# Reordered SwiGLU forward pass, other DMA queues and moved PSUM copies in a fused recurrent-attention and SwiGLU training step

## The chip, the core and the metric

The kernel runs on one core of a Trainium2 chip. The metric is the device time of one execution in microseconds (us): 5259.43 us, the median of three runs of the kernel before (5244.72 to 5269.86). The profiled execution has a span of 5258.0 us; all windows below are counted from its start.

Names: PE is TensorE, DVE is VectorE, ACT is ScalarE, POOL is GpSimd, SP is SyncE. SP, ACT and POOL start the DMA transfers; "the sync queue" is that of SP, "the scalar queue" that of ACT, "the GpSimd queue" that of POOL.

## What is computed

A training step: the output of one layer and the gradients of all its inputs. Cut to what matters:

```python
def f(x, mem0, Wq, Wk, Wv, Wo, w1, w3, w2):
    xn = layernorm(x)                       # 2048 x 640
    s = A(xn, mem0, Wq, Wk, Wv, Wo)         # recurrent attention
    g = silu(B(xn, w1, w3, w2))             # SwiGLU, hidden width 1728
    return x + s * g

def A(x, mem, ...):                         # 64 segments of 32 tokens, 32 heads of 128
    for seg in x:
        h = concat(mem, seg)                # 8 + 32 rows
        o = Wo(softmax(mask(q(h) @ k(h).T)) @ v(h))
        mem, out = o[:8], o[8:]             # the memory goes on to the next segment

def B(x, w1, w3, w2):
    return (silu(x @ w1) * (x @ w3)) @ w2

out, vjp = jax.vjp(f, ...)                  # returned: out and vjp(grad_out), nine gradients
```

All arrays are bfloat16. The 64 segments are a chain in both directions: each step of the forward and of the backward loop needs the 8 memory rows of the step before it.

## The kernel before

[...] The stages, in time: layer norm and SwiGLU forward (with the first V rows at its end), the first K and Q rows, the forward loop, a projection stage, the lead-in of the backward loop, the backward loop, and the weight gradients.

SwiGLU forward: four blocks of 512 tokens. `hidden` makes one 128-row chunk of the hidden layer (14 to a block), `up` the output rows of the block before.

```python
def fetch(blk):                     # 512 normalised rows, turned by DMA on the sync queue
    xnT = io.tile([P, DC, BLK], BF16, name="xnT_b", tag="xnT_b")
    for i in range(2):
        turned_load(k, xnT[...], k.XN[...])
    xnTs.append(xnT)

def hidden(blk, fc):
    pg = ps.tile([P, BLK], F32, name="pg", tag="pg")     # 2 PSUM buffers each
    pu = ps.tile([P, BLK], F32, name="pu", tag="pu")
    ...                                                   # 5 + 5 matmuls of 128x512
    sig = wk.tile(...)                                    # pool wk: bufs=2
    nc.scalar.activation(sig[:fsz], pg[:fsz], ACT.Sigmoid)
    nsig = wk.tile([P, BLK], BF16, name="nsig", tag="nsig", bufs=1)
    nc.scalar.activation(nsig[:fsz], pg[:fsz], ACT.Sigmoid, scale=-1.0)
    ut = wk.tile(..., bufs=3)
    nc.scalar.copy(ut[:fsz], pu[:fsz])
    sl = wk.tile(..., bufs=3)
    nc.vector.tensor_tensor(sl[:fsz], pg[:fsz], sig[:fsz], ALU.mult)
    nc.vector.tensor_tensor(hBT[:fsz, fc, :], sl[:fsz], ut[:fsz], ALU.mult)
    ds = wk.tile(..., bufs=3)
    nc.vector.tensor_tensor(ds[:fsz], nsig[:fsz], sl[:fsz], ALU.mult)
    nc.vector.tensor_tensor(ds[:fsz], sig[:fsz], ds[:fsz], ALU.add)
    nc.gpsimd.dma_start(k.SLT[...], sl[:fsz])
    nc.gpsimd.tensor_tensor(ds[:fsz], ds[:fsz], ut[:fsz], ALU.mult)
    nc.gpsimd.dma_start(k.DUT[...], ds[:fsz])

def hidden_out(blk):                # the whole hidden block, 1.7 MB
    nc.gpsimd.dma_start(k.HB[...], hBT[:, 0:FC - 1, :]) ...
```

The layer norm of the last three quarters of the rows (`ln_stats`, `ln_rstd`, `ln_rows`) is done between the chunks of block 0.

The first K and Q rows: 48 groups of two 112x512 tiles, with a copy by DVE and one by ACT into one staging tile of 224 KB, and a store of it. The weights Wq and Wo are loaded meanwhile on the scalar queue.

```python
# pool b0s: bufs=2
def first_rows(k, ps, stage, xs, off, W, dst, x0, cg, ...):
    for b in range(2):
        ...                                              # 5 matmuls of 112x512
        k.copy(st[:, s0:s0 + 512], pb[:], eng='vs'[b])   # 'v' is DVE, 's' is ACT
        if w == 512 or b == 1:
            nc.sync.dma_start(dst[...], st[:])
```

The fold that ends each step of both loops (the projection's partial sums lie in two halves of one PSUM bank), and what stands around it in the backward loop:

```python
def fold_add(k, pm, pool, lo="flo"):
    up = pool.tile([64, 160], F32, name="fup", tag="fup")
    nc.scalar.copy(up[:], pm[64:128, 0:160])
    lw = pool.tile([64, 160], F32, name="flo", tag=lo)
    nc.vector.tensor_copy(lw[:], pm[0:64, 160:320])
    nc.vector.tensor_tensor(fs[:, 0:160], pm[0:64, 0:160], up[:], ALU.add)
    nc.vector.tensor_tensor(fs[:, 160:320], pm[64:128, 160:320], lw[:], ALU.add)

WARM = dict(G4=1, G5=1)             # matmuls without use, to keep PE from pausing

def chain(t, gap):                  # one backward step; gap(...) puts other work in
    packed_half(k, bA, gox, WoT, 0)                      # 20 matmuls
    k.copy(sg[:, 0:512], bA[:], eng='s')
    packed_half(k, bB, gox, WoT, 1)
    k.copy(sg[:, 512:1024], bB[:], eng='v')
    packed_sel(k, pg, sg, 0)
    gap("W0")                                            # turn(t, 0): 8 transposes, 3 ACT copies
    packed_sel(k, pg, sg, 1)
    ...                                                  # gmT <- pg, two DVE copies
    gap("W1")                                            # turn(t, 1)
    for a in range(2):
        nc.tensor.transpose(pgo[:, a, :], gmT..., k.ident[:])
    nc.scalar.copy(gOst[:], pgo[:])
    dprob_m(0)                                           # 16 small matmuls
    gvT = gkv(1, gOst, bdP)                              # 2 matmuls with gOst, DVE
    ...
    fs = fold_add(k, pm, ch, "gstg")
    gap("G4")
    pt = fold_turn(k, bC, fs)                            # 6 small matmuls
    gap("G5")
    nc.vector.tensor_copy(goxs[(t - 1) % 2][:, :, 0:8], pt[:])   # what the next step starts from
```

The lead-in of the backward loop goes through 19 units of the same side work before the loop starts; in it the sync queue also turns Wq (5.2 MB, four DMA transposes) and two tiles of GS.

Of the kernel before, what the change touches and what calls it, by code (L numbers as in the profile page):

```python
# [16 lines left out]
P = 128  # L17
# [312 lines left out]
def fold_add(k, pm, pool, lo="flo"):  # L330

    nc = k.nc
    fs = pool.tile([64, 320], BF16, name="fsum", tag="fsum")
    up = pool.tile([64, 160], F32, name="fup", tag="fup")
    nc.scalar.copy(up[:], pm[64:128, 0:160])
    lw = pool.tile([64, 160], F32, name="flo", tag=lo)
    nc.vector.tensor_copy(lw[:], pm[0:64, 160:320])
    nc.vector.tensor_tensor(fs[:, 0:160], pm[0:64, 0:160], up[:], ALU.add)
    nc.vector.tensor_tensor(fs[:, 160:320], pm[64:128, 160:320], lw[:], ALU.add)
    return fs  # L340
# [19 lines left out]
def first_rows(k, ps, stage, xs, off, W, dst, x0, cg, nb=112, tag="b0pb", w=1024):  # L360

    nc = k.nc
    for b in range(2):
        c0 = cg * 1024 + b * 512
        if w == 512 or b == 0:
            st = stage()
        pb = ps.tile([nb, 512], F32, name="b0pb", tag=tag)
        for dc in range(k.DC):
            nc.tensor.matmul(pb[:], xs[:, dc, x0 - off:x0 - off + nb], W[:, dc, c0:c0 + 512],
                             start=(dc == 0), stop=(dc == k.DC - 1))  # L370
        s0 = b * 512 if w == 1024 else 0
        k.copy(st[:, s0:s0 + 512], pb[:], eng='vs'[b])
        if w == 512 or b == 1:
            nc.sync.dma_start(dst[x0:x0 + nb, cg * 1024 + (b * 512 if w == 512 else 0):cg * 1024 + b * 512 + 512], st[:])
# [21 lines left out]
def first_part(k, Wv, Wk_, Wq, Wo, kTs, vt, hxs, rest):  # L396
    nc, tc = k.nc, k.tc
    DC, H, HD = k.DC, k.H, k.HD
    with tc.tile_pool(name="b0", bufs=1) as io, tc.tile_pool(name="b0s", bufs=2) as stp, \
# [9 lines left out]
        for i, tt in enumerate(kTs + hxs + rest + [vt]):  # L409
            nc.gpsimd.memset(tt[:], 0.0)  # L410
        nc.gpsimd.dma_start(k.m_rows(k.HRO, 0), k.mem0)
# [21 lines left out]
        for W, dst in ((Wk_, k.KX[:, :]), (Wq, k.QVX[:, 0])):  # L433
            for x0 in range(0, k.NB0, 112):
                for cg in range(4):
                    if n % 2 == 0 and fetch:
                        nc.scalar.dma_start(*fetch.pop(0))
                    first_rows(k, ps, lambda: stp.tile([112, 1024], BF16, name="b0st", tag="b0st"), xs, 0, W, dst, x0, cg)
                    if n >= 26 and n % 2 == 0 and (n - 26) // 2 < 9:
                        i = (n - 26) // 2  # L440
                        if i > 0:
                            kturn(i - 1)
                        if i < 8:
                            kload(i)
                    if n == 44:
                        for i in range(2):
                            nc.sync.dma_start(vt[64 * i + 8:64 * i + 40, :], k.QVX[0:32, 1, 2048 * i:2048 * i + 2048])
                    n += 1
# [511 lines left out]
def phase4_Abwd(k, out2, WoT, WvT, WkT, WqT, later):  # L960
# [3 lines left out]
    with tc.tile_pool(name="gst", bufs=1) as st, tc.tile_pool(name="gchain", bufs=1) as ch, \  # L964
# [25 lines left out]
        WARM = dict(G4=1, G5=1)  # L990
# [53 lines left out]
        def chain(t, gap):  # L1044
# [20 lines left out]
            k.copy(sg[:, 0:512], bA[:], eng='s')  # L1065
            packed_half(k, bB, gox, WoT, 1)
            k.copy(sg[:, 512:1024], bB[:], eng='v')
# [13 lines left out]
            nc.scalar.copy(gOst[:], pgo[:])  # L1081
# [68 lines left out]
        def ld(tl, qd, eng=None):  # L1150
# [17 lines left out]
            (nc.gpsimd if early else nc.sync).dma_start(  # L1168
                qv[nx:n], k.QVM[t0:t0 + ns, :, qd // 2, :, 512 * (qd % 2):512 * (qd % 2) + 512].rearrange("t r i c -> (t r) i c"))
            k.load_x(qv, 0, k.x_src(tl, "qv", c0, c0 + 512), nc.sync)  # L1170
            k.load_x(gor, 0, k.g_src(tl, c0, c0 + 512), nc.scalar if early and i > 3 else nc.sync)
            nc.sync.dma_start(Pr[0:n], k.PR[tl][:, h0:h0 + 4, :])
# [46 lines left out]
        def gmem(tl, qd):  # L1219
# [12 lines left out]
            nc.gpsimd.dma_start(k.GXP[tl, :, qd, 0:ns], ks[:].rearrange("p s i h m -> p s i (h m)"))  # L1232
# [393 lines left out]
def phase12_ln_Bfwd(k: K, Wv, Wk_):  # L1626
# [6 lines left out]
    with tc.tile_pool(name="bw", bufs=1) as wp, tc.tile_pool(name="bio", bufs=2) as io, \  # L1633
# [29 lines left out]
        def ln_rows(tt):  # L1663
            xt = xts.pop(tt)
            nc.vector.tensor_scalar(xt[:], xt[:], mv[:, tt, 0:1], k.rstd_all[:, tt:tt + 1], op0=ALU.subtract, op1=ALU.mult)
            nc.gpsimd.dma_start(k.XN[tt * P:(tt + 1) * P, :], xt[:])
# [3 lines left out]
        def fetch(blk):  # L1670
            xnT = io.tile([P, DC, BLK], BF16, name="xnT_b", tag="xnT_b")
            for i in range(2):
                turned_load(k, xnT[:, :, i * BLK // 2:(i + 1) * BLK // 2], k.XN[blk * BLK + i * BLK // 2:blk * BLK + (i + 1) * BLK // 2, :])
            xnTs.append(xnT)

        def hidden(blk, fc):
# [11 lines left out]
            nsig = wk.tile([P, BLK], BF16, name="nsig", tag="nsig", bufs=1)  # L1688
# [3 lines left out]
            sl = wk.tile([P, BLK], BF16, name="sl", tag="sl", bufs=3)  # L1692
            nc.vector.tensor_tensor(sl[:fsz], pg[:fsz], sig[:fsz], ALU.mult)
            nc.vector.tensor_tensor(hBT[:fsz, fc, :], sl[:fsz], ut[:fsz], ALU.mult)
            ds = wk.tile([P, BLK], BF16, name="ds", tag="ds", bufs=3)
            nc.vector.tensor_tensor(ds[:fsz], nsig[:fsz], sl[:fsz], ALU.mult)
            nc.vector.tensor_tensor(ds[:fsz], sig[:fsz], ds[:fsz], ALU.add)
            nc.gpsimd.dma_start(k.SLT[fc * P:fc * P + fsz, cols], sl[:fsz])
# [3 lines left out]
        def up_ld(blk, ti):  # L1702
            tt = TB * blk + ti
            Gt = wk.tile([P, D], BF16, name="Gt", tag="Gt")
            nc.scalar.dma_start(Gt[:], k.G[tt * P:(tt + 1) * P, :])
# [35 lines left out]
        for w, src in ((w1s, k.w1), (w3s, k.w3)):  # L1741
            nc.scalar.dma_start(w[:, :, 0:512], src.rearrange("(dc p) f -> p dc f", p=P)[:, :, 0:512])
        for tt in range(TB):
# [4 lines left out]
        fetch(0)  # L1748
        for w, src in ((w1s, k.w1), (w3s, k.w3)):
            nc.sync.dma_start(w[:, :, 512:F], src.rearrange("(dc p) f -> p dc f", p=P)[:, :, 512:F])  # L1750
        for tt in range(TB, 3 * TB):
            ln_ld(tt)
        nc.scalar.dma_start(w2s[:, 0:FC - 1, :], k.w2[0:(FC - 1) * P, :].rearrange("(c p) d -> p c d", p=P))
        nc.scalar.dma_start(w2s[0:fszs[-1], FC - 1, :], k.w2[(FC - 1) * P:F, :])
        for blk in range(NBLK):
            for fc in range(FC):
                hidden(blk, fc)
                if blk in (1, 2) and fc % 3 == 1:
                    W, src = ((Wv, k.A_Wv), (Wk_, k.A_Wk))[blk - 1]
                    nc.scalar.dma_start(W[:, fc // 3, :], src.rearrange("(dc p) h e -> p dc (h e)", p=P)[:, fc // 3, :])  # L1760
                if blk == 0:
                    g, m = fc // 4 + 1, fc % 4
                    if g < 4:
                        if m < 2:
                            ln_stats(TB * g + 2 * m)
                            ln_stats(TB * g + 2 * m + 1)
                        else:
                            if m == 2:
                                ln_rstd(TB * g, TB * g + TB)
                            ln_rows(TB * g + 2 * m - 4)  # L1770
                            ln_rows(TB * g + 2 * m - 3)
                        if fc == 3:
                            for tt in range(3 * TB, NT):
                                ln_ld(tt)
                    if fc == 9:
                        fetch(1)
                    if fc == 13:
                        k.x_rows(k.HRO, k.XN, nc.sync)
                elif fc == 0:
                    hidden_out(blk - 1)  # L1780
                    for ti in range(2):
                        up_ld(blk - 1, ti)
                elif fc < 9 and fc % 2 == 0:
                    up(blk - 1, fc // 2 - 1)
                    if fc < 6:
                        up_ld(blk - 1, fc // 2 + 1)
                elif fc == 9:
                    fetch((blk + 1) % NBLK)
        hidden_out(NBLK - 1)
# [292 lines left out]
```

## Time and profile before

| stage | window, us | length, us | PE busy, us | DMA share |
|---|---|---|---|---|
| layer norm, SwiGLU forward until its first matmul | 0 to 24 | 24 | 0.30 | 0.78 |
| SwiGLU forward, four blocks | 24 to 264 | 240 | 184.07 | 0.73 |
| last `up` rows and first V rows, wait for the next stage | 264 to 350 | 86 | 68.47 | 0.46 |
| first K and Q rows | 350 to 484 | 134 | 116.09 | 0.55 |
| forward loop and its tail | 484 to 1878 | 1394 | 1215.11 | 0.52 |
| projection stage | 1878 to 1994 | 116 | 107.50 | 1.00 |
| lead-in of the backward loop | 1994 to 2136 | 142 | 53.23 | 0.80 |
| backward loop | 2136 to 3340 | 1204 | 1081.87 | 0.65 |
| weight gradients and the rest | 3340 to 5258 | 1918 | 1793.13 | 0.58 |

The table is from the view of busy time by window. PE busy is the sum of the matmul records in the window, which overlap one another a little; DMA share is the mean busy share of the core's 16 DMA engines. A row is read by the distance between its length and PE's busy time: where they lie close, PE sets the pace of the stage; where they lie apart, something else makes PE wait, and the view of waits for that window says what.

### The profile page before, as it was taken

How to read it: one execution, taken by the hardware profiler on the slowest of the kernel's cores; microseconds unless marked ns; L12 is line 12 of the kernel's file. 1: busy time of each engine (PE TensorE's matmuls, PEld its weight loads, DVE VectorE, ACT ScalarE, POOL GpSimd, SP SyncE). 2: the span in 40 equal slices, each digit the busy share in tenths (PEclk: the TensorE clock that was granted, in tenths of full speed). 3: DMA queues.
4: the chain of work that ended last, by engine and by line, in shares of the span. 5: the costliest groups of instructions: out<-in, count | busy, mean ns of one | idle time of the engine just before them, and what ended most of it. 6: DMA issues, size and time to landing. Idle time of an engine off the chain costs nothing. (4 is left out here: it accounts for less than half of the span.)

```text
span 5258.0 us, 160316 instructions
## 1 busy us (share of the span) xinstructions
PE 4619.8 (88%) x64317; PEld 2931.1 (56%) x64587; DVE 2241.9 (43%) x7236; ACT 1691.0 (32%) x4828; POOL 1960.6 (37%) x3309
## 2 busy tenths in 40 slices
PE   5778888888889874789999999789999999999999
PEld 2445555555555452455555555556665566657675
DVE  6623555555565522444444454323332233311361
ACT  3422455555555431223333333212322223200000
POOL 5620344444444402344444444423442334401340
PEclk9899999999999886899999999899999999999999
DMA  7754555555555488566776666645654355549783
GB/s 220 198 161 128 146 158 162 164 162 158 160 156 159 134 177 166 164 192 191 197 200 186 189 191 170 142 100 127 144 123 101 100 131 141 131 138 239 169 197 94
DMA packets 1042847, 836.70 MB, mean 159 GB/s; under 512 B 596361, under 2 KB 925005, under 8 KB 1040099
## 3 DMA queue, kind: packets, MB, share of 16 engines
q1 hardware_dynamic: 813748, 538.36, 39.3%
q0 software_dynamic: 125488, 222.36, 15.2%
q10 hardware_dynamic: 102867, 65.71, 4.9%
q8 instruction: 510, 8.36, 0.7%
q14 instruction: 234, 1.92, 0.1%
HBM read 463.32 MB, written 306.24 MB: 146 GB/s over the span
## 5 line engine op out<-in xcount | busy, mean ns | idle before, releaser
L1474 PE MATMUL wg<-gr,hr 128*128 128x512 bf16 x2352 | 525.3, 382 | 20.8 <-DVE dST L1398 14.5
L1453 PE MATMUL g<-w,ghacc 128*128 128x320 bf16 x3072 | 450.5, 305 | 0.0
L1474 PEld LDWEIGHTS <-hr 128*128 128x128 bf16 x2400 | 235.6, 98 | 302.7 <-issue 29.1
L1453 PEld LDWEIGHTS <-ghacc 128*128 128x128 bf16 x3072 | 299.4, 100 | 116.0
L306 PEld LDWEIGHTS <-hx 128*32 128x32 bf16 x7680 | 182.8, 98 | 175.2 <-issue 23.1
L713 POOL DMA_DIRECT2D OR<-xv x163 | 92.7, 569 | 483.7 <-ACT xv L712 378.9
L90 DVE CAST wgo<-wg 128x512 bf16<-128x512 f32 x72 | 47.5, 688 | 525.2 <-issue 249.8
L90 DVE CAST stg<-bank 128x512 bf16<-128x512 f32 x256 | 177.1, 692 | 199.4 <-PE bank L306 194.1
L325 PEld LDWEIGHTS <-gkv 128*8 128x8 bf16 x8192 | 188.2, 92 | 103.9 <-issue 3.0
L664 ACT ACTIVATE xP<-xsp,xnm 120x120 bf16<-120x120 f32 (+1 forms) x704 | 240.6, 376 | 8.4 <-DVE xnm L660 5.1
L1185 POOL DMA_DIRECT2D VTD<-gvT x176 | 129.6, 743 | 297.2 <-ACT gvT L1184 262.1
L1422 POOL DMA_DIRECT2D GSP<-grs x48 | 25.6, 538 | 523.0 <-ACT grs L1414 507.8
L92 ACT CAST wgo<-wg 128x512 bf16<-128x512 f32 x48 | 25.8, 589 | 573.3 <-PE wg L1474 573.3
L325 PE MATMUL gbank<-WvT,gkv 128*8 128x320 bf16 x4096 | 208.0, 358 | 0.2
L675 POOL TENSOR_TENSOR xP<-xP,xrz 120x480 bf16<-120x480 bf16 x163 | 161.8, 993 | 117.8 <-ACT xP L664 79.2
L1462 DVE TENSOR_TENSOR ghacc<-ghacc,g 128x320 f32<-128x320 f32 x192 | 93.7, 488 | 238.3 <-PE g L1453 238.3
L1414 ACT CAST gr<-r6p 120x512 bf16<-120x512 f32 x160 | 94.0, 587 | 302.0 <-PE r6p L1407 300.8
L1214 DVE SCALAR_TENSOR_TENSOR gdS<-gdp,Dx,gPr 120x120 bf16<-120x120 f32 (+1 forms) x680 | 183.0, 332 | 0.0
L325 PE MATMUL bank<-Wo,oTm 128*32 128x320 bf16 x4032 | 182.0, 336 | 0.3 <-DVE oTm L582 0.2
L1232 POOL DMA_DIRECT2D GXP<-gks x176 | 102.5, 582 | 208.8 <-ACT gks L1230 200.9
L243 POOL DMA_DIRECT2D r<-GOS x256 | 144.5, 568 | 71.8 <-PE r6p L1407 21.9
L539 DVE COPY vt<-stg 8x512 bf16<-8x512 bf16 x512 | 161.9, 316 | 20.9 <-ACT stg L92 13.2
(339 smaller groups left out, 10968.1 us busy)
## 6 DMA issues: line engine op xcount, KB each, us to landing
QVS<-stg SPq DMA_DIRECT2D x128, 256.0 KB
gqv<-QVS SPq DMA_DIRECT2D x108, 192.0 KB
vTt<-VTD SPq DMA_DIRECT2D x64, 320.0 KB
VTD<-gvT POOLq DMA_DIRECT2D x168, 120.0 KB, 4.0
DSR<-gdS POOLq DMA_DIRECT2D x168, 120.0 KB, 3.4
dS<-DSR SPq DMA_DIRECT2D x168, 120.0 KB
P<-PR SPq DMA_DIRECT2D x168, 120.0 KB
gPr<-PR SPq DMA_DIRECT2D x164, 120.0 KB
```

The lines of the kernel that those rows point to most:

```text
L90: return nc.vector.tensor_copy(out, in_)
L243: eng.dma_start(d, src if src.shape[0] > 1 else src[0])
L306: k.nc.tensor.matmul(bank[32 * g:32 * g + 32, :], x[:, dc, :], W[:, dc, c0:c0 + 512], start=(dc == 0), stop=(dc == k.DC - 1), tile_positio ...
L325: k.nc.tensor.matmul(pm[p0:p0 + nq, 0:320], x[:, h, :], W[:, h, 320 * b:320 * b + 320], start=(first and i == 0), stop=(last and i == 15), ...
L539: nc.vector.tensor_copy(vt[p0:p0 + 8, c0:c0 + 512], sv[32 * g:32 * g + 8, b * 512:(b + 1) * 512])
L664: nc.scalar.activation(Pb[0:n, j, 0:n], sp[0:n, j, :], ACT.Exp, bias=nmx[0:n, j:j + 1], scale=k.scale, accum_out=Z[0:n, j:j + 1])
L675: eng.tensor_tensor(Pb[0:n, :, 0:n], Pb[0:n, :, 0:n], bc_last(rz[0:n], n), ALU.mult)
L1185: nc.gpsimd.dma_start(k.VTD[tl][:, :, h0:h0 + 4, :], vTq[:])
L1214: nc.vector.scalar_tensor_tensor(dS[0:n, j, 0:n], dp[0:n, j, :], Dx[0:n, j:j + 1], Pr[0:n, j, 0:n], op0=ALU.subtract, op1=ALU.mult)
L1232: nc.gpsimd.dma_start(k.GXP[tl, :, qd, 0:ns], ks[:].rearrange("p s i h m -> p s i (h m)"))
L1453: nc.tensor.matmul(pg[:], ring[:, i, j, r0:r0 + P], Ws[qd][i][:, j, 320 * h:320 * h + 320], start=(i == 0 and j == 0), stop=(i == 2 and j ...
L1474: nc.tensor.matmul(accs[dc][:], hr[:, tl, dc * P:(dc + 1) * P], grs[i][:, tl, :], start=(tl == 0), stop=(tl == NF - 1))
```

## The change

The change has five parts.

1. **SwiGLU forward.** The first block's rows are turned by PE (`turn_first`) and copied by ACT instead of being stored and turned by DMA. The layer norm of a block is done in the block ahead of it, for all blocks, instead of all in block 0. `nsig` gets two buffers, `sl` and `ds` four. The stores of `sl`, and the loads of w2, Wv, Wk and G, go to the sync queue; the stores of `ds` and of the hidden block stay on the GpSimd queue.
2. **First K and Q rows.** Three staging tiles instead of two, the stores on the GpSimd queue, and most of the clearing of tiles by POOL moved from ahead of the stage to between its stores.
3. **fold_add.** One ACT copy of 320 columns replaces an ACT copy and a DVE copy of 160 each.
4. **Backward loop.** The two copies of `sg` change engines, `gOst` is copied by DVE, and the unused matmul at G5 is gone.
5. **Lead-in.** Its loads of Q, V and P rows go to the GpSimd queue, its loads of `gor` all to the sync queue, its stores of GXP to the sync queue.

The aim is to take waits of PE away at the start of the kernel and in the chains of both loops.

```diff
-def fold_add(k, pm, pool, lo="flo"):
+def fold_add(k, pm, pool, tag="fup"):
-    up = pool.tile([64, 160], F32, name="fup", tag="fup")
-    nc.scalar.copy(up[:], pm[64:128, 0:160])
-    lw = pool.tile([64, 160], F32, name="flo", tag=lo)
-    nc.vector.tensor_copy(lw[:], pm[0:64, 160:320])
-    nc.vector.tensor_tensor(fs[:, 0:160], pm[0:64, 0:160], up[:], ALU.add)
-    nc.vector.tensor_tensor(fs[:, 160:320], pm[64:128, 160:320], lw[:], ALU.add)
+    up = pool.tile([64, 320], F32, name="fup", tag=tag)
+    k.nc.scalar.copy(up[:], pm[64:128, 0:320])
+    for c in (0, 160):
+        k.nc.vector.tensor_tensor(fs[:, c:c + 160], pm[0:64, c:c + 160], up[:, c:c + 160], ALU.add)
 ... first_part
-    tc.tile_pool(name="b0s", bufs=2) as stp
+    tc.tile_pool(name="b0s", bufs=3) as stp
-        for i, tt in enumerate(kTs + hxs + rest + [vt]):
+        for tt in hxs:
             nc.gpsimd.memset(tt[:], 0.0)
+        zero = [kTs[0]] + [vt, kTs[1]] + rest
-                    first_rows(k, ps, ..., xs, 0, W, dst, x0, cg)
+                    first_rows(k, ps, ..., xs, 0, W, dst, x0, cg, q=nc.gpsimd)
+                    if zero:
+                        nc.gpsimd.memset(zero.pop(0)[:], 0.0)
 ... backward loop
-        WARM = dict(G4=1, G5=1)
+        WARM = dict(G4=1)
-            k.copy(sg[:, 0:512], bA[:], eng='s')
+            k.copy(sg[:, 0:512], bA[:], eng='v')
-            k.copy(sg[:, 512:1024], bB[:], eng='v')
+            k.copy(sg[:, 512:1024], bB[:], eng='s')
-            nc.scalar.copy(gOst[:], pgo[:])
+            nc.vector.tensor_copy(gOst[:], pgo[:])
 ... its lead-in
-            (nc.gpsimd if early else nc.sync).dma_start(
+            q = nc.gpsimd if early else nc.sync
+            q.dma_start(
                 qv[nx:n], k.QVM[...])
-            k.load_x(qv, 0, k.x_src(tl, "qv", c0, c0 + 512), nc.sync)
-            k.load_x(gor, 0, k.g_src(tl, c0, c0 + 512), nc.scalar if early and i > 3 else nc.sync)
-            nc.sync.dma_start(Pr[0:n], k.PR[tl][:, h0:h0 + 4, :])
+            k.load_x(qv, 0, k.x_src(tl, "qv", c0, c0 + 512), q)
+            k.load_x(gor, 0, k.g_src(tl, c0, c0 + 512), nc.sync)
+            q.dma_start(Pr[0:n], k.PR[tl][:, h0:h0 + 4, :])
-            nc.gpsimd.dma_start(k.GXP[...], ...)
+            (nc.sync if (tl, qd) in pro else nc.gpsimd).dma_start(k.GXP[...], ...)
 ... SwiGLU forward
+        def turn_first():
+            xnT = io.tile([P, DC, BLK], BF16, name="xnT_b", tag="xnT_b")
+            for tt in range(TB):
+                pt = ps.tile([P, DC, P], BF16, name="lnpt", tag=("pg", "pu")[tt % 2])
+                for dc in range(DC):
+                    nc.tensor.transpose(pt[:, dc, :], xts[tt][:, dc * P:(dc + 1) * P], k.ident[:])
+                nc.scalar.copy(xnT[:, :, tt * P:(tt + 1) * P], pt[:])
+            xnTs.append(xnT)
-            nsig = wk.tile([P, BLK], BF16, name="nsig", tag="nsig", bufs=1)
+            nsig = wk.tile([P, BLK], BF16, name="nsig", tag="nsig")
-            sl = wk.tile(..., bufs=3)
+            sl = wk.tile(..., bufs=4)
-            ds = wk.tile(..., bufs=3)
+            ds = wk.tile(..., bufs=4)
-            nc.gpsimd.dma_start(k.SLT[...], sl[:fsz])
+            nc.sync.dma_start(k.SLT[...], sl[:fsz])
-        fetch(0)
+        turn_first()
-        nc.scalar.dma_start(w2s[:, 0:FC - 1, :], ...)     # ahead of block 0
+                if blk == 0 and fc == 5:
+                    nc.sync.dma_start(w2s[:, 0:FC - 1, :], ...)
-                if blk == 0:
-                    ...                                   # layer norm of blocks 1 to 3, 4 chunks each
-                    if fc == 9:
-                        fetch(1)
-                    if fc == 13:
-                        k.x_rows(k.HRO, k.XN, nc.sync)
+                g = blk + 1
+                if g < NBLK:
+                    ...                                   # layer norm of block g, chunks 0 to 3
+                if fc == 9:
+                    fetch((blk + 1) % NBLK)
+                if blk == 3 and fc == 2:
+                    k.x_rows(k.HRO, k.XN, nc.sync)
```

## The prediction

> **What bounds the kernel now.** I read the page first: PE is busy 88% of the span, so a change pays only where PE waits. The busy time by window then shows where that is. Columns: window, its length, busy us (and instructions) of PE, weight loads, DVE, ACT, POOL, then the granted PE clock, the DMA share and GB/s.
>
> ```profile
> span 5258.0 us, 160316 instructions
> ```
>
> ```profile
> core 0: us, PE busy (x) PEld busy (x) DVE busy (x) ACT busy (x) POOL busy (x), PEclk, DMA share, GB/s
> 0.00:24.00 24.00, 0.30 (x1) 0.21 (x2) 7.62 (x27) 2.86 (x3) 5.94 (x26) 1.00 0.78 238
> 24.00:264.00 240.00, 184.07 (x879) 90.97 (x894) 155.46 (x316) 111.10 (x198) 152.53 (x215) 0.91 0.73 206
> 350.00:484.00 134.00, 116.09 (x520) 67.28 (x524) 35.41 (x56) 27.67 (x48) 8.81 (x11) 0.93 0.55 166
> 1994.00:2136.00 142.00, 53.23 (x529) 31.53 (x536) 39.90 (x249) 27.57 (x104) 49.40 (x86) 0.59 0.80 162
> 2136.00:3340.00 1204.00, 1081.87 (x24305) 686.33 (x24369) 567.34 (x2840) 365.20 (x1233) 507.99 (x925) 0.95 0.65 181
> ```
>
> The reader is to see that PE is not the whole of the first 264 us, that the lead-in of the backward loop (1994 to 2136) is far from PE-bound with DMA at 0.80, and that the backward loop is PE-bound but for some 120 us. Next, PE's waits up to 484 us, then those in the backward loop (total, times, longest):
>
> ```profile
> PE pg L1684 <- DVE sl L1693: 54.7, 26, 11.5
> PE pg L1684 <- DMA xnT_b<-XN: 23.7, 1, 23.7
> PE b0pb L369 <- DVE b0st L90: 22.7, 12, 4.2
> PE b0pb L369 <- DMA b0x<-XN: 9.6, 1, 9.6
> ```
>
> ```profile
> PE gbank L355 <- DVE fsum L338: 52.4, 63, 6.6
> PE gbank L1055 <- ACT gOst L1081: 38.4, 59, 0.8
> PE gbank L314 <- DVE gstg L90: 13.1, 63, 0.6
> ```
>
> PE waits for sl; why is sl late? The waits of DVE and of ACT in 24 to 264 us answer:
>
> ```profile
> DVE sl L1693 <- DMA SLT<-sl: 31.1, 7, 9.0
> DVE sl L1693 <- ACT nsig L1689: 30.1, 30, 14.8
> ```
>
> ```profile
> ACT nsig L1689 <- DVE ds L1696: 64.4, 38, 9.5
> ```
>
> nsig has one buffer, so it waits for the ds of the chunk before; sl has three, and its store stands on the GpSimd queue behind the hidden block (HB, 18.5 us to landing in the DMA view). Last, the order of a fold in the timeline of one backward step (start, length; idle before):
>
> ```profile
> 2708.38 0.29 ACT L335 COPY fup<-gbank 64x160 f32<-64x160 f32 x1 [1.88 <-PE gbank L325]
> ```
>
> ```profile
> 2708.70 0.32 DVE L337 COPY flo<-gbank 64x160 f32<-64x160 f32 x1 [2.35 <-ACT fup L335]
> 2708.94 0.30 DVE L338 TENSOR_TENSOR fsum<-gbank,fup 64x160 bf16<-64x160 f32 x1
> ```
>
> The two copies were meant to run side by side; they run one after the other.
>
> [...] DVE's copy waits for ACT's copy of the same bank (228.8 us in 90 cases, both loops)[...]. [...] GS, a small tile, is waited for 14.7 us at 2072 us behind a turn of Wq. [...] The trace shows five 128x512 matmuls taking 2.29 us after a 4.2 us pause and 1.24 us otherwise, so a long wait costs about 2 us on top.
>
> **The change part by part.**
>
> *SwiGLU forward.* Matmuls start at 23.7 us, as rows are stored, landed and turned by DMA. The last rows are normalised by DVE at 12.3 us. With PE's transposes, an ACT copy of 128x640 of about 0.7 us (that is what sz, L1719, takes) and semaphores, I put the first matmul at 14 us: **-10 us**. From then on a chunk costs PE 2.16 us (two groups of five, 1.08 us apart) and an `up` 3.80 us. Block 0 is 14 x 2.16 = 30.2 us of PE, a later block 30.2 + 4 x 3.80 = 45.4. The timeline has the blocks starting at 23.7, 78.5, 143.2 and 206.1 and the V rows at 264.5: 240.8 us against 30.2 + 3 x 45.4 = 166.4. DVE takes 1.88 us a chunk in the timeline when undisturbed, 26.3 a block, plus some 7 for a block's layer norm and 9 for `up`: 42, just under PE. So a later block can come close to 45.4, not below. I allow each 8.6 us more, for layer norm delaying DVE, for ds behind HB (three buffers cost 11.8 us, four will not cost nothing) and for the sl stores, which now stand behind the turned loads on the sync queue; and 6.8 us in block 0. V rows start at 14 + 37 + 3 x 54 = 213: **-52 us** in all, with the start. The V rows themselves and the 9.6 us wait that follows them are not touched.
>
> *First K and Q rows.* 48 groups x 2.16 = 103.7 us of PE; the stage takes 134. PE waits 17.4 us in it for staging copies (8 times), which wait for stores (45.7 us of DVE idle), all while Wq and Wo load; slow clock after the pauses is about 10. A third tile lets a store take a group longer. The loads still take DMA time, and POOL's clearing of kT (3.3 us each) now stands between stores, so I take half: **-12 us**.
>
> *fold_add.* ACT takes 0.289 us for 160 columns and 0.587 for 512, so 320 is estimated at 0.289 + 160 x 0.00085 = 0.425. First add after ACT's start: before 2708.94 - 2708.38 = 0.56, after 0.425 + 0.03 = 0.455. The second add follows the first as now. 0.10 x 127 steps: **-6 us** forward, **-6 us** backward. PE waits for the fold in every step, so it is on the path.
>
> *Backward loop.* gOst: the transposes end at about 2714.88, ACT starts its copy at 2715.37 because six copies of the two turns come first, and PE idles 0.46 us to 2715.86. DVE has finished gmT at 2714.60. Its copies of 128x128 and 128x384 bf16 take 0.23 and 0.36 us, so 0.29 here: gOst is there by 2715.25, before PE is through with dprob_m(0) at 2715.40. The wait goes; of its 38.4 us I count 35: **-35 us**. sg's second half: ACT's 0.59 for DVE's 0.69, 0.10 x 63: **-6 us**. The matmul at G5: gox is copied by 2710.45, the next step starts at 2710.66 behind the unused matmul; without it at about 2710.51, 0.15 x 63: **-9 us**. DVE is at 567 of 1204 us and can take 64 x 0.29 more.
>
> *Lead-in.* 142 us at DMA 0.80 is 114 us of all 16 engines; no queue makes that smaller. Loads of V and P no longer stand behind the turns of Wq, but gor and the GXP stores do, and the store of GX (13 us waits of DVE on its one gstg) shares the GpSimd queue with more. I count **-5 us**.
>
> Sum: -52 - 12 - 6 - 6 - 35 - 6 - 9 - 5 = -131 us, 5259 - 131 = 5128. Sums of this kind tend to be given back in part, so 5135.
>
> **The rivals.** (1) *DMA becomes the bound of SwiGLU forward.* 0 to 264 us has 0.78 x 24 + 0.73 x 240 = 194 us of DMA time. Less the first turned block (about 10) that is 184 us in a stage I want in 213: 0.86. If a block waits for its turned rows or for stores, the gain there is 25 instead of 52: 5160. For it: the shares of 0.80 to 0.87 in the blocks that load Wv and Wk. Against it: nothing in the waits of PE but the first load was a DMA. (2) *The loop's gain turns into a wait of DVE or ACT.* If PE then waits for gmT or gox instead, half of the 50 us stays: 5160. Against it: both were ready well ahead in the step above. (3) *The lead-in slows*, since the sync queue is held by turns of Wq for 5 to 9.6 us each and GXP has two buffers: 10 to 20 us more, 5150 to 5155. (4) *A lower granted clock* when PE pauses less: 0.91 to 0.95 leaves room both ways; 1% in the two loops would be 26 us.
>
> **Range and chances.** Two rivals together give 5190; everything full, with the first blocks at PE's own pace, is 5259 - 131 - 33 = 5095. So 5085 to 5195. The 2% line lies at 5154, 19 us above the middle: 0.68 below, 0.30 within, 0.02 slower, as no part adds work to the path.
>
> **What would show it.** First matmul at 14 us, later blocks at 50 to 56 us, no wait of sl for the SLT store; K and Q rows in about 122 us; DVE's add starting 0.45 us after ACT's fold copy; no PE wait on gOst and a step of about 17.9 us for 18.8; the lead-in at 130 to 145 us. Wrong would be: a later block above 58 us with DMA near 0.95, a new wait of PE on DVE in the backward step, or a lead-in well above 150 us. The 1918 us after 3340 us must not change.

## The result, and the profile after

The changed kernel takes 5053.21 us (median of four runs, 5040.95 to 5062.48) against 5252.08 us of the kernel before beside it (four runs, 5230.94 to 5269.86): a ratio of 0.9621, 95% interval 0.9578 to 0.9665. That is 199 us less; the prediction had 124 less, and a range that ended at 5085. It erred by being too small.

The profiled execution of the changed kernel has a span of 5039.3 us. Its busy time by window, columns as in the prediction; the rows answer to those shown of before (start, SwiGLU forward, K and Q rows, backward loop), each at its new place:

```profile
0.00:14.00 14.00, 2.54 (x20) 1.99 (x21) 7.61 (x27) 4.08 (x6) 5.94 (x26) 1.00 0.91 326
14.00:209.00 195.00, 174.55 (x895) 88.62 (x895) 160.03 (x316) 111.55 (x201) 122.76 (x160) 0.98 0.77 254
295.00:413.00 118.00, 109.80 (x516) 65.12 (x520) 35.78 (x56) 27.52 (x48) 38.11 (x59) 0.97 0.57 186
2013.00:3106.00 1093.00, 1038.33 (x24034) 674.63 (x24027) 558.36 (x2830) 348.06 (x1163) 506.41 (x921) 0.98 0.71 199
```

Read the third column from the right first. The granted PE clock was 0.91 in SwiGLU forward, 0.93 in the K and Q rows and 0.95 in the backward loop; it is now 0.98, 0.97 and 0.98. The backward loop of before, cut at the last step's first matmuls as here:

```profile
2136.00:3326.00 1190.00, 1069.66 (x24027) 679.14 (x24094) 563.99 (x2829) 363.42 (x1227) 506.69 (x923) 0.95 0.66 183
```

PE's busy time there (the time in which at least one matmul is on record) fell from 1070 us to 1038, with 24027 matmuls on record before and 24034 after: they ran faster. The prediction has no term for that.

PE's waits (total, times, longest) in four answers: SwiGLU forward of the changed kernel, its K and Q rows, the same rows of the kernel before, and the backward loop of the changed kernel:

```profile
PE pg L1694 <- DVE sl L1703: 17.2, 11, 6.5
...
PE pg L1694 <- DMA xnT_b<-XN: 1.2, 1, 1.2
```

```profile
PE b0pb L366 <- DVE b0st L90: 7.5, 4, 3.2
```

```profile
PE b0pb L369 <- DVE b0st L90: 17.4, 8, 4.2
```

```profile
PE gbank L352 <- DVE fsum L336: 27.2, 63, 3.2
...
PE gbank L314 <- ACT gstg L92: 2.1, 4, 0.5
...
PE gbank L1055 <- DVE gOst L1081: 0.3, 1, 0.3
```

The wait for sl fell from 54.7 to 17.2 us, that for turned rows from 23.7 to 1.2 (the first block is no longer among them), staging from 17.4 to 7.5. In the loop gOst fell from 38.4 to 0.3 and gstg from 13.1 to about 2. The fold's 52.4 and 27.2 can't be compared as they stand: the unused matmul ahead of the fold has no records in before, and a missing record counts as wait. With all its records the row is 34.9 us with the former fold (b_gost, below) and 27.2 after; without them it is 52.4 and 40.7 (a second profile of the changed kernel).

Where the span went, by stage. A stage starts at its first matmul in the trace; "half" is the time within it in which the records of the granted clock show half speed. The two profiled executions are 218.7 us apart.

```
stage            before: us   half     after: us   half     gain   predicted
start                  23.7    0.0          14.1    0.0      9.6      52, with
SwiGLU forward        240.8   41.0         195.3    6.8     45.5      the start
first V rows           85.8    7.6          86.2    9.7     -0.4       0
K and Q rows          133.4   19.7         117.2    7.3     16.2      12
forward loop         1321.4  109.2        1277.9   44.4     43.5       6
tail, projections     197.2   79.1         193.3   69.0      3.9       0
lead-in               134.2  110.3         128.6  108.1      5.6       5
backward loop        1189.6  124.5        1093.0   38.0     96.6      56
weight gradients     1931.8  119.5        1933.6  121.5     -1.8       0
```

Everything outside the loops is within 5 us of its term. The two loops are 78 us beyond theirs, and they are where half-clock time fell most, by 65 and 86 us.

### The profile page after: what moved, and what is told of

Its sections match the earlier page's. It is cut to its first block, busy times and chain, and to the rows that moved or that the text cites. A ratio compares the mean times of both kernels' runs of the same rounds, so it can differ in the third digit from the quotient of the medians.

```text
span 5039.3 us, 160411 instructions
## 1 busy us (share of the span) xinstructions
PE 4576.7 (91%) x64544; PEld 2909.6 (58%) x64544; DVE 2213.2 (44%) x7173; ACT 1685.0 (33%) x4768; POOL 1968.3 (39%) x3320
## 5 line engine op out<-in xcount | busy, mean ns | idle before, releaser
L1423 POOL DMA_DIRECT2D GSP<-grs x48 | 25.6, 537 | 517.9 <-ACT grs L1415 502.6
L325 PE MATMUL gbank<-WvT,gkv 128*8 128x320 bf16 x4096 | 171.8, 312 | 0.2 <-issue 0.2
L306 PE MATMUL gbank<-WoT,gox 128*32 128x512 bf16 x2560 | 153.9, 387 | 18.3 <-POOL gox L1005 12.2
L1233 POOL DMA_DIRECT2D GXP<-gks x157 | 91.7, 584 | 201.8 <-ACT gks L1231 190.1
```

Source lines behind the costliest of these rows:

```text
L306: k.nc.tensor.matmul(bank[32 * g:32 * g + 32, :], x[:, dc, :], W[:, dc, c0:c0 + 512], start=(dc == 0), stop=(dc == k.DC - 1), tile_positio ...
L325: k.nc.tensor.matmul(pm[p0:p0 + nq, 0:320], x[:, h, :], W[:, h, 320 * b:320 * b + 320], start=(first and i == 0), stop=(last and i == 15), ...
```

## The experiments

Two theories for the loops. **Chain**: what the steps wait for became shorter than I had counted, and nothing else. **Clock**: besides that, the short waits that vanished had been making the clock drop to half, and PE now runs its other matmuls faster. The prediction gave the clock only to long waits.

To tell them apart, the tables below give the **full-clock step** beside the stage: the median distance of two steps' first matmuls, over steps 9 to 60, of those steps in which no half-clock record lies. That is the chain without the clock.

**1. One part at a time in the kernel before, and matmuls alone.** b_fold:

```diff
-    (before's fold_add: ACT copies 160 columns, DVE copies 160, two adds)
+    (after's fold_add: ACT copies 320 columns, two adds)
```

> The kernel before with the new fold_add alone. Chain theory (the fold is shorter by what the timelines of before and after show, 0.22 us from the last matmul to the last of the six small ones): forward loop -14 us, backward loop -14 us, in all about -28 us, the granted PE clock of the loops as before (0.96 and 0.95). Clock theory (a shorter wait also keeps PE's clock from being halved): forward loop -35 to -45 us with its clock at 0.98; backward loop -14 to -35 us, since the wait for gOst is still there and can still halve the clock; in all -50 to -80 us.

b_gost:

```diff
-            nc.scalar.copy(gOst[:], pgo[:])
+            nc.vector.tensor_copy(gOst[:], pgo[:])
```

> The kernel before with the copy of gOst on DVE alone. Chain theory: the step is shorter by the wait of 0.7 us, backward loop about -43 us, clock there still 0.95. Clock theory: backward loop -55 to -80 us and its clock at 0.97 or more. Both: nothing in the forward loop (within 10 us), which this edit doesn't touch.

b_warm shortens no wait; it puts unused 128x512 matmuls into three of them:

```diff
-        WARM = dict(G2=1, G3=1, G4=2, G5=1)      # forward
+        WARM = dict(G2=1, G3=1, G4=2, G5=4)
-        WARM = dict(G4=1, G5=1)                  # backward
+        WARM = dict(G4=4, G5=1)
             dprob_m(0)
+            for _ in range(3):
+                nc.tensor.matmul(bA[:], k.ident[:], WqT[:, 0, 0:512], start=True, stop=True)
             gvT = gkv(1, gOst, bdP)
```

> The kernel before with unused 128x512 matmuls put into the waits: three more for each fold in both loops, and three ahead of the matmuls that need gOst. No copy is moved and no chain is shorter, the steps only keep PE busy while it would wait. Chain theory: 0 to +15 us. Clock theory: forward loop -20 to -40 us and backward loop -25 to -45 us, clock of both at 0.98, in all -45 to -85 us.

b_ffn is the kernel before with the whole SwiGLU part of the change and nothing else:

> The kernel before with the changed SwiGLU forward alone. Both theories: first matmul at 14 us, V rows from about 209 us instead of 264, in all -50 to -58 us; loops within 10 us of before. A rival, that moving the early stages also changes what the loops meet (data in flight, clock), would show as more than 10 us in a loop.

Times beside 5241.15 us of the kernel before, and the loops of their profiles:

```
          median   ratio, 95% interval        forward      backward     full-clock     of 52 steps,
              us                               us   half    us    half   step backward  touched by half clock
before         -   -                       1321.4  109  1189.6    125       17.91          27
b_fold    5207.30  0.9933 (0.9911-0.9954)  1280.0   55  1161.9     97       17.69          21
b_gost    5164.63  0.9852 (0.9835-0.9869)  1300.7   65  1106.7     25       17.38           2
b_warm    5194.44  0.9906 (0.9884-0.9928)  1291.9   48  1157.6     27       18.03           3
b_ffn     5176.23  0.9877 (0.9853-0.9901)  1295.6   51  1190.0    125       17.91          28
```

b_warm decides it. Its backward step is 0.12 us *longer* at full clock, as extra work must make it, and yet its backward loop is 32 us shorter, because 3 of 52 steps are touched by half clock and not 27. The row of its backward loop:

```profile
2100.00:3257.00 1157.00, 1123.71 (x24460) 696.97 (x24464) 563.73 (x2829) 362.49 (x1227) 506.11 (x922) 0.99 0.67 188
```

The clock is 0.99 where it was 0.95. That is 98 us less at half clock. b_gost shortens the step by 0.53 us, which is 33 us for 63 steps, but its loop by 83: with it go 100 us at half clock. Its 76 us by the medians were what the clock theory expected, not the chain's 43; b_warm's 47 likewise. b_fold's 34 lie between the two theories: 0.22 us a step of chain, twice the prediction's term, and 28 us less at half clock. The price can be read from before alone: its 25 undisturbed steps have a mean of 18.01 us, the 27 touched ones 19.88 with 3.79 us of half clock in each, 0.49 us for each us at half clock. Chance does not explain these differences: in four profiles that leave the backward loop alone (b_ffn and three below) it took 1187.5 to 1200.8 us, with 122 to 133 us at half clock.

In the forward loop the four must be read with care. b_gost and b_ffn don't touch it, and it still took 1300.7 and 1295.6 us, not 1321.4; so b_ffn's 26 us there, which its rival would have taken for an effect, and b_warm's 29.5 are not shown to be gains. (b_ffn's median is 65 us below before; 56 are the start and SwiGLU forward of its profile.) In five profiles with that loop unchanged (b_gost, b_ffn and three below) it took 1295.6 to 1303.0 us with 51 to 68 us at half clock. The 109 us of before's own profile were an unlucky draw, worth about 20 us. b_fold's 1280.0 against those 1300 is 16 to 23 us gained in the forward loop.

**2. The same step undone in the changed kernel.** a_base is the changed kernel once more. a_gostact gives gOst back to ACT. a_gostwarm does that too, and fills the wait that returns:

```diff
-            nc.vector.tensor_copy(gOst[:], pgo[:])      # a_gostact, a_gostwarm
+            nc.scalar.copy(gOst[:], pgo[:])
             dprob_m(0)
+            for _ in range(3):                          # a_gostwarm alone
+                nc.tensor.matmul(bA[:], k.ident[:], WqT[:, 0, 0:512], start=True, stop=True)
             gvT = gkv(1, gOst, bdP)
```

> The changed kernel again, unaltered, as the base for the three that run beside it. 5040 to 5065 us and 0.958 to 0.967 of the kernel before. If chance in the granted clock is as large as the forward loop's three unchanged runs suggest (1296 to 1321 us), the stage lengths of this profile differ from those of the first by up to 15 us in each loop, and by the half-clock time at 0.44 us a microsecond.

> The changed kernel with gOst copied by ScalarE again, all else as changed. Chain and clock theory: the wait of TensorE comes back (about 0.6 us a step, 39 us in the backward loop) and with it the half-clock windows, some 60 us more of them at 0.44: 60 to 90 us over the changed kernel. Chain alone: 35 to 45 us over it, with no more half-clock windows than the changed kernel has (38 us).

> As a_gostact, with three unused 128x512 matmuls (0.69 us) put where TensorE waits for gOst, so gOst is as late as in a_gostact but TensorE is busy meanwhile. Chain and clock theory: half-clock windows stay as few as in the changed kernel (under 50 us of them), and the backward loop is 25 to 45 us below a_gostact, 30 to 50 us over the changed kernel. Chain alone: the same as a_gostact or up to 10 us more, since nothing waits less.

The 0.44 us for each us at half clock, here and in two expectations below, was the author's estimate; before's steps give 0.49.

Beside 5241.32 us of the kernel before:

```
             median   ratio, 95% interval       backward     full-clock   of 52 steps,
                 us                              us    half   step         touched by half clock
a_base      5069.59  0.9673 (0.9648-0.9699)  1103.1     42    17.03           3
a_gostact   5134.03  0.9795 (0.9777-0.9813)  1177.7    116    17.75          27
a_gostwarm  5100.76  0.9732 (0.9715-0.9750)  1152.1     36    17.75           2
```

This is the cleanest pair. a_gostact and a_gostwarm have the same full-clock step, 17.75 us: three matmuls fit into the wait and lengthen nothing. But with PE idle in it 27 of 52 steps meet half clock, with PE busy in it 2. The backward loop, first of a_gostact and then of a_gostwarm:

```profile
2022.00:3199.00 1177.00, 1058.48 (x23952) 684.35 (x24019) 539.68 (x2766) 365.33 (x1226) 507.04 (x922) 0.95 0.65 185
```

```profile
2026.00:3177.00 1151.00, 1051.44 (x24082) 687.29 (x24204) 539.79 (x2767) 365.51 (x1226) 506.52 (x921) 0.98 0.68 189
```

The second has the more work for PE and the less busy time. PE's waits in the two loops, in the same order:

```profile
PE gbank L1055 <- ACT gOst L1081: 48.9, 58, 1.0
```

```profile
PE gbank L1055 <- ACT gOst L1081: 7.0, 37, 0.2
```

The wait is still there, filled. So of the 74.6 us that a_gostact's loop lost against a_base, 25.6 come back by work that nobody uses: clock. The remaining 49 are chain (0.73 us x 63 = 46). Chain alone had expected nothing to come back. By the medians 33 us come back; a_gostwarm's profile has one stop of 12.5 us in its loop, whose releaser it doesn't show, and a_gostact's has none like it. a_base itself came out a little above its expectation, 5069.6 for 5065. Its backward loop, 10 us longer than the first profile's with the same step, has a single stop of 15.8 us in one step, whose releaser the profile doesn't show; it was 3.6 there.

**3. The fold undone in the changed kernel** (a_oldfold: before's fold_add, everything else as changed).

> The changed kernel with the former fold (ScalarE copies 160 columns, VectorE copies 160 and adds twice). The prediction's own term: 0.10 us a step, 12 to 13 us over the changed kernel in both loops. The fold as the trace now shows it (0.22 us a step, 64 and 63 steps) with the clock at 0.3 to 0.44 us for each us at half clock: 14 us of chain and 5 to 15 us of clock in each loop, 35 to 60 us over the changed kernel; half-clock windows of the backward loop 60 to 100 us for 38 to 42.

5084.75 us against 5238.27, ratio 0.9698 (0.9682 to 0.9714). Its forward loop took 1300.2 us against 1281.6 of a_base, its backward loop 1108.2 against 1103.1, with half clock as in a_base (65 and 39 us). The full-clock backward step is 17.20 against 17.03. So 24 us in the two loops (its median is 26 us above that of a_nsig1, measured beside it and, as shown below, no slower than the changed kernel), below the 35 to 60 expected and above the term's 13: the chain is there, 0.18 us a step backward and 0.2 or more forward, but undoing it brought no further half clock. Here a longer wait did not cost clock; this one alone was not enough.

**4. The first K and Q rows alone** in the kernel before (b_kq):

```diff
-    tc.tile_pool(name="b0s", bufs=2)          +    tc.tile_pool(name="b0s", bufs=3)
-    nc.sync.dma_start(dst[...], st[:])        +    nc.gpsimd.dma_start(dst[...], st[:])
-    (kT, vt and rest cleared ahead)           +    (one of them cleared after each group)
```

> The kernel before with the K and Q rows' part alone (third staging buffer, stores on the GpSimd queue, kT and vt cleared between). If the third buffer is what counts, the stage takes 116 to 124 us for 133 and TensorE's wait for staging copies (17.4 us) falls under 6; if it was the earlier loads of the SwiGLU part, the stage stays at 128 to 134. In all 9 to 17 us less, or 0 to 5.

The stage took 119.2 us, half clock 8.3 for 19.7; PE's wait for staging was 9.1 us for 17.4, not under 6. 5230.45 us against 5238.27, ratio 0.9984 (0.9969 to 0.9998): the stage gains 14 us by itself, about as predicted, while the whole gains 8, just under the 9 to 17 expected. Which of the three edits does it, the third buffer, the queue or the later clearing, the run doesn't separate.

**5. SwiGLU forward: which part of the edit?** The prediction blamed nsig's one buffer and the queue of the sl stores. Six runs, each with one piece of the edit undone in the changed kernel (a_) or done alone in the one before (b_):

```diff
a_nsig1   -nsig: bufs=2                              +nsig: bufs=1
a_slt     -nc.sync.dma_start(k.SLT[...], ...)        +nc.gpsimd.dma_start(k.SLT[...], ...)
a_ln0     -layer norm of block g beside block g - 1  +all of it beside block 0
a_actq    -Gt, Wv, Wk on nc.sync, w2 at chunk 5      +all on nc.scalar, w2 ahead of block 0
b_nsig2   -nsig: bufs=1                              +nsig: bufs=2
b_slt     -sl: bufs=3, stores on nc.gpsimd           +sl: bufs=4, stores on nc.sync
```

> The changed kernel with one nsig buffer again. If ScalarE's nsig waiting for the ds of the chunk before is what held sl back, as the prediction has it, TensorE's waits for sl return, 15 to 30 us more in the SwiGLU stage (210 to 225 us for 195). If the stores and their order were the cause, it stays within 5 us of 195.

> The changed kernel with the sl stores on the GpSimd queue again, behind HB and the ds stores, four buffers as changed. If the queue is what made sl wait for its store (31 us in 7 waits before), the SwiGLU stage takes 5 to 15 us more than 195 and the wait of VectorE's sl for its store is back at 10 us or more; if the fourth buffer alone was enough, within 3 us of 195.

> The changed kernel with the layer norm of blocks 1 to 3 all beside block 0 again, as before, everything else as changed. If moving VectorE's work is what shortened the SwiGLU stage: VectorE's busy time beside block 0 rises from 24 to about 44 us, block 0 takes 42 to 55 us for 30, later blocks 48 to 53 for 54 to 56, the stage 203 to 220 us for 196. If the placing doesn't matter because the later blocks give back what block 0 loses: within 4 us of 196.

> The changed kernel with the loads of Wv, Wk, G's rows and w2 on ScalarE's queue again, w2 ahead of block 0 as before. If those loads on ScalarE's queue (its copies and sigmoids behind them, or w2 beside the first block's rows) held the SwiGLU stage, it takes 205 to 225 us for 196; if not, within 4 us of 196.

> The kernel before with two nsig buffers and nothing else. If the single buffer is what held sl back before, as the prediction says, the SwiGLU stage takes 210 to 228 us for 241 (233 to 248 in the five profiles of kernels that leave it alone). If it was only where ScalarE happened to wait: 230 to 248, and ScalarE's 64 us wait for ds is gone without gain.

> The kernel before with the sl stores on the sync queue and a fourth sl buffer, nothing else. If the sl stores behind HB were the larger part of the 45 us, the SwiGLU stage takes 205 to 222 us for 241 (233 to 248 where it is left alone); if they were worth the 10 us that a_slt gave back, 225 to 238, and VectorE's 31 us wait for the store is gone.

```
          SwiGLU stage   against             median   ratio, 95% interval
a_nsig1      195.6 us    195.3, 196.2 after  5058.80  0.9650 (0.9632-0.9669)
a_ln0        200.8                           5056.83  0.9656 (0.9636-0.9676)
a_slt        206.1                           5067.89  0.9665 (0.9650-0.9680)
a_actq       216.5                           5074.79  0.9680 (0.9645-0.9715)
b_nsig2      237.3       240.8 before        5234.97  0.9994 (0.9983-1.0005)
b_slt        235.1                           5229.04  0.9973 (0.9962-0.9983)
```

The stages are of one profile each. Seven profiles that leave the changed stage alone have 194.3 to 197.8 us.

The nsig story falls on both sides. These are waits in a_nsig1's SwiGLU stage, of ACT and then of DVE:

```profile
ACT nsig L1699 <- DVE ds L1706: 55.2, 40, 11.3
```

```profile
DVE sl L1703 <- ACT nsig L1699: 13.7, 33, 5.3
```

ACT's great wait is back, 55.2 us in 40 times, and the stage is not a microsecond longer. ACT is busy 111.6 of the stage's 195 us in the changed kernel; that row was idle time of an engine that isn't the bottleneck, and I had read it as a cause. In b_nsig2 the wait is gone, and the stage is within the 233 to 248 us it takes when left alone.

What counts more is where loads and stores are queued. With the sl stores back on the GpSimd queue (a_slt) sl waits for them again, and less than before with its fourth buffer:

```profile
DVE sl L1703 <- DMA SLT<-sl: 8.1, 2, 6.2
```

10 us of the stage. With the weights' and G's loads on ACT's own queue (a_actq), DVE waits for ACT, though ACT's sigmoids wait no longer for ds than in the changed kernel (17.6 us for 17.7), and PE waits for the turned rows:

```profile
DVE sl L1703 <- ACT nsig L1699: 27.3, 8, 9.3
```

```profile
PE pg L1694 <- DMA xnT_b<-XN: 14.7, 2, 11.0
```

20 us, the largest piece. Two waits make up most of the 27.3: 8.4 us end at 20.5 us, after the issue of the second w2 load had kept ACT for 4.57 us, and 9.3 end at 122 us, just behind PE's 11.0 for turned rows. So w2's place ahead of block 0 has a share in it; how much is the queue's, the run doesn't separate. The layer norm's place gives 5: DVE is busy 43.7 of block 0's 50.3 us in a_ln0 and 33.0 of 41.0 in the changed kernel, but the later blocks give most back, 47 us each for 49. Of the 45.5 us of the stage 35 are so accounted for if the pieces add; the rest isn't split further. The clock runs through all of them: the stage has 34 us less at half clock than before, which at the loop's 0.49 would be 17 us (an estimate), and a_actq has 14 us more of it than the changed kernel. The pieces needn't add: in the kernel before, b_slt cured its wait and gained 6 us, within the 233 to 248 us that this stage takes when left alone. DVE's waits for stores and PE's for the turned rows in b_slt:

```profile
DVE ds L1696 <- DMA DUT<-ds: 28.9, 5, 11.5
...
DVE sl L1693 <- DMA SLT<-sl: 3.8, 1, 3.8
```

```profile
PE pg L1684 <- DMA xnT_b<-XN: 36.8, 2, 23.6
```

Of sl's 31.1 us for its store 3.8 are left, but ds now waits 28.9 us for its own store, for 11.8 before. And beside the start's wait for turned rows, 23.6 of the 36.8 us, there is a second one of 13.2 us, at 210 us, where the last block begins. That is what the prediction's first rival had feared, in a kernel that makes only part of the edit.

**6. A version that goes further.** The forward loop still loses 44 us at half clock. Its waits repeat with the step's place among three (in the changed kernel's trace PE's gaps over 0.15 us add up to 1.35, 1.38 or 1.86 us by the median, from one add of the fold to the next), so a_warm puts as many unused matmuls into each as it holds:

```diff
-        WARM = dict(G2=1, G3=1, G4=2, G5=1)
+        WARM = [dict(G2=4, G3=2, G4=2, G5=3), dict(G1=1, G2=1, G3=2, G4=2, G5=3),
+                dict(G1=2, G2=3, G3=2, G4=2, G5=1)]
-                for i in range(WARM.get(g, 0)):
+                for i in range(WARM[t % 3].get(g, 0)):
```

> The changed kernel with one to three more unused matmuls in each of the forward loop's waits, as many as the wait of that kind of step holds. Clock theory: the forward loop's 44 us of half clock fall under 15, and with 0.44 us for each the loop is 10 to 20 us shorter than in the changed kernel (5030 to 5045 us in all). Chain alone: 0 to 10 us longer, since the matmuls only take TensorE's time. The backward loop is untouched.

5040.24 us (five runs, 5038.36 to 5070.22) beside a_base's 5069.59; ratio to before 0.9631 (0.9607 to 0.9656) against 0.9673 (0.9648 to 0.9699). The intervals just overlap. In the profile the forward loop took 1270.3 us for 1281.6 and 1277.9, with 10 us at half clock for 61 and 44, and none in steps 9 to 60. The gain per us at half clock, 0.22, is less than half of the backward loop's price. Part of that is the matmuls' own cost: the full-clock step of the forward loop grew from 19.96 and 19.98 us to 20.06. And in this loop the touched steps of the same two profiles show a price of only 0.31 and 0.33. PE's longest wait left in it:

```profile
PE bank L352 <- DVE fsum L336: 20.5, 62, 0.6
```

It was 33.2 us in the changed kernel's first profile. The median is the lowest measured here, but the ratio is no lower than that of the changed kernel's first measurement, 0.9621: that the whole kernel is faster is not shown.

## Why the prediction was wrong, point by point

**SwiGLU forward and start: -52, measured -55.** The first matmul is at 14.1 us (14), the V rows start at 209.4 (213). b_ffn alone puts them at 208.3. The sum was right and partly luck: block 0 took 41.0 us and the next three 49.5, 49.3 and 55.5, where I had 37 and three times 54. And the cause was half wrong: not nsig, but the loads on ACT's queue with w2's early place, and, in part, the sl stores, as named. What remains as waits is what I had allowed for, ds behind HB:

```profile
DVE ds L1706 <- DMA DUT<-ds: 11.7, 3, 9.5
...
DVE sl L1703 <- DMA SLT<-sl: 0.5, 2, 0.3
```

(DVE's waits from 14 to 209 us in the changed kernel.) Rival 1 did not come: DMA at 0.77, PE waits 1.2 us for turned rows.

**K and Q rows: -12, measured -16.** Right; "I take half" was a little cautious.

**fold_add: -6 and -6. The term was mis-sized.** The timeline of one backward step after (start, length; idle before):

```profile
2537.50 0.42 ACT L334 COPY fup<-gbank 64x320 f32<-64x320 f32 x1 [2.87 <-PE gbank L325]
2537.96 0.55 DVE L336 TENSOR_TENSOR fsum<-gbank,fup 64x160 bf16<-64x160 f32 x2 [3.47 <-ACT fup L334]
```

ACT's copy was put at 0.425 us and takes 0.42; the first add was put at 0.455 after ACT's start and comes at 0.46. Then the step that failed: "the second add follows the first as now". Two adds now take 0.55 us together, and the second starts 0.24 us after the first, where it started 0.34 after it before. (It now reads the same 64 rows of the PSUM bank as the first; before it read the other 64. Whether that is why, no run here shows.) The last of the small matmuls behind them comes 1.42 us after ACT's start for 1.64: 0.22 us a step, not 0.10. In the full-clock step it is 0.18 to 0.22, in both loops 24 us (a_oldfold) for 12. The prediction also put 228.8 us down to DVE's copy waiting for ACT's of the same bank. That figure is all of DVE's idle time ahead of the copy, most of it spent while PE was still at work; in the timeline the copy starts 0.32 us after ACT's, which is the most that this order can have cost in that step.

**Backward loop, chain: -35 - 6 - 9 - 6 = -56; the full-clock step says -56.** It fell from 17.91 to 17.02 us, 0.89 x 63. That the sums agree is luck in part, for the terms were not these: gOst is worth 0.53 (b_gost) to 0.73 us (a_gostact) where I had 0.56, the fold 0.2 for 0.1, and for sg's second half and the matmul at G5 together 0.14 at most is left, for the 0.25 I had; no run has either of the two alone. Rival 2 did not come: PE waits 1.3 us for gox and 1.5 for gmT.

**The clock: no term; some 40 us in the backward loop.** The prediction wrote "a step of about 17.9 for 18.8". 17.9 was what the step before took *at full clock*; the 18.8 held about a microsecond of slow matmuls, and the change removed both 0.9 us of chain and most of that. With 0.49 us for each us at half clock, 86.5 us less of it is 42 us, and 56 + 42 = 98 of the 96.6 measured. The step that failed is "a long wait costs about 2 us on top": it took the price from a 4.2 us pause and gave it to long pauses only. (Its own figures, 2.29 and 1.24 us, make 1.05, not 2.) Rival 4 had the clock in hand, 0.95 with "1% in the two loops" worth 26 us, but named the wrong sign: PE paused less here and was granted more, 0.98.

**Forward loop: -6, measured -43.5.** Three things: the fold, 8 to 15 us at the 0.12 to 0.24 us by which the full-clock steps differ in the mean (before to changed, a_oldfold to a_base); about 20 us of chance in before's profile; and the rest, put down to the clock, which no pair of runs isolates in this loop. Against the 1295.6 to 1303.0 us of the unchanged loop in other profiles the gain is 18 to 25; nine profiles with the changed fold have 1277.9 to 1291.1. The chance also lies in the result: the changed kernel measured again is 172 us below before (a_base), not 199. Even so the prediction's 124 was too small, by about the clock.

**Lead-in -5, measured -5.6; weight gradients unchanged to 1.8 us.** The lead-in's agreement is luck: it takes 128.4 to 137.1 us in the eight profiles that leave it alone and 127.2 to 136.1 in the ten that have its change (134.1 in a_base), and no run has that part by itself. Rival 3 did not come. The weight gradients are as written.

## What to carry to other kernels

Before pricing a wait of TensorE in a loop, split the loop's steps into those with and without a half-clock record: the difference of their means is the price of the clock, and removing a wait may be worth more than its length (here 0.53 us a step, 33 us in all, brought 83). If a wait can't be removed, unused matmuls that just fit in it can get the clock's part back, as in b_warm and a_gostwarm (98 and 80 us less at half clock in the backward loop), and a pair of kernels with and without them separates clock from chain. Read another engine's large wait as a cause only after asking whether that engine has time to spare: ACT's 64 us for nsig were free (without that wait, in b_nsig2, the stage took 237.3 us, within the 233 to 248 us it takes when left alone).

## What the hardware showed that I had not expected

In the clock records of both traces, half clock comes in stretches of 3.413 us or whole multiples, to within 0.006 us: 98 of the 99 stretches before, 48 of the 49 after. Their starts lie on one grid of 3.413 us through the whole execution, to within 0.009 us. Whether the chance in the loops comes from where a step's waits fall on this grid, no run here shows.

With before's backward loop cut into windows at this grid, 109 full-clock windows had PE's matmuls in under 0.82 of the window (by the records, some of which are missing), and 31 of them were followed by a half-clock window; of the 202 busier ones 2 were. So emptier windows went ahead of 31 of the 33 changes to half clock, and their gaps were mostly short: in 26 of the 33 the longest recorded gap was 0.74 or 0.75 us, in 6 of these with a second one of 0.17 or 0.18. But the busy share alone does not sort them. Of 31 windows with a single gap of about 0.75 us, at gOst, 20 were followed by half clock; of 14 with recorded gaps of 0.98 and 0.18 us around the fold none was, though they were the emptier even when the missing unused matmul (0.38 us) is counted in. What decides, no run here shows.
